# Carrying the softmax sums of a two-branch attention kernel by DMA, with paired V products and a new static order

## The chip, the cores and the metric

The kernel runs on one core of one Trainium2 chip. The metric is the device time of one execution in microseconds (us). Engines: PE is TensorE (matmul), PEld its weight loads, DVE is VectorE, ACT is ScalarE, POOL is GpSimd, SP is SyncE, which here only issues DMAs. Every ratio below is the mean time of one kernel's fast runs over the mean of the other's fast runs of the same rounds on the same chip, so it is not quite the ratio of the medians that are quoted. On one core a run counts as "slow" when it lies more than 1.5% above the fastest run of the same kernel. Such runs are left out of the ratios; where they matter I say how many there were. Here the slow runs are mostly those with the most time at half clock, so leaving them out can favour the kernel that has more of them.

## The reference, cut to what matters

```python
def reference(A_x, A_wqkv, A_w_phi, A_wo, B_x, B_wqkv, B_wo, gate_w):   # S=2048, D=512, 32 heads of 16
    # branch A: linear attention with a softmax feature map, per head
    phi_q = concat([softmax(q @ w_phi), softmax(-(q @ w_phi))]);  phi_k the same of k
    o_A = (phi_q @ (phi_k.T @ v)) / (phi_q @ sum(phi_k) + 1e-6)
    # branch B: ordinary softmax attention, 32 heads, 2048 x 2048 scores each
    p = softmax((q @ k.T) * 16 ** -0.5);  o_B = p @ v
    g = sigmoid((x * gate_w).sum(-1, keepdims=True))
    return g * (o_A @ A_wo) + (1 - g) * (o_B @ B_wo)                        # x = A_x in both branches
```

The cost is branch B: 32 blocks (4 query chunks x 8 head groups), each of 64 score tiles of 128 x 512, 2048 tiles in all. Every score has to go through an exponential.

## The kernel before: the parts that matter

The program is a list of operations with dependencies, estimated durations and priorities. Code in the kernel (`layout`) lays them out in time when the program is built, and each engine then gets its instructions in that fixed order, with semaphore waits only for true dependencies.

Most score tiles are exponentiated by ACT, in calls of two or three PSUM banks. 416 of them (`DN` per block) are instead approximated on DVE by integer arithmetic, in groups of four: D1 evicts each score tile from PSUM with the exponent bits in place, D2 and D3 split mantissa and exponent bits, D4 multiplies; in 32 of the 104 groups D4 runs on POOL (the range below names 34 numbers, two of which lie beyond the last group):

```python
ACTIVE = (0.64, 0.66, 0.60, 0.54)            # PE activity below which filler matmuls are planned
POOL_GROUPS = tuple(range(8, 110, 3))        # groups whose D4 runs on POOL
...
    add(0.72, lambda e: e.tensor_scalar(... 0x007F, 0x3F00, bitwise_and, bitwise_or), ..., "D2", ...)
    add(0.72, lambda e: e.tensor_single_scalar(... 0x7F80, bitwise_and), ..., "D3", ...)      # ops[-1].lock = True
    if g["n"] not in POOL_GROUPS:
        add(1.24, lambda e: e.tensor_tensor(t, t, m, ALU.mult), ..., "D4")
    else:
        for q in range(4):
            ops.append(P.add("pool", 1.0, ..., lambda e, q=q: e.tensor_tensor(quarter(t, q), ...), ...))
            ops[-1].lock = True
```

When the plan finds that PE streamed matmuls for less than a share `ACTIVE` of the last 3.4 us, it puts one or two filler matmuls, whose result nobody reads, in front of the next score product:

```python
    if op.room and t > 20.0 and active < ACTIVE[1]:
        op.extra = min(op.room, 1 if active > ACTIVE[2] else 2)
        ...
    elif op.tight and t > 20.0 and active < ACTIVE[3]:
        op.extra = 1
...
    def fn(e):                                # a score product for one exponential call
        for _ in range(op.extra):
            e.matmul(psS[:, ...], lhsT=ident[:], rhs=xT[:, 0, 0:NQ], start=True, stop=True)   # filler
        for m, t in enumerate(ts):
            ins = qk_mm(e, t, psS[:, ...])
```

The V products of a block collect in PSUM bank `psO`, with the sum of weights as one more row (a column of ones in `vaug`). At the end of each block DVE transposes the bank, takes a reciprocal, multiplies, and after every second block transposes back:

```python
    P.add("dve", 0.69, -50, lambda e: e.transpose(Tf[:, bb, :], psO[:]), ...)
    P.add("dve", 0.25, -40, lambda e: e.reciprocal(rd[:, bb, :], tv[:, :, DH]), ...)
    P.add("dve", 0.48, -40, lambda e: e.tensor_tensor(tbv, tv[:, :, 0:DH], rd..., ALU.mult), ...).lock = True
    if par == 1:
        P.add("dve", 0.72, -40, lambda e: e.transpose(oT[:, qc % 2, r, :], TB[:]), ...)
```

The softmax here doesn't subtract the row's maximum and nothing guards it: scores larger than these inputs give would overflow.

## Time and profile before

| | before |
|---|---|
| median of the first 3 runs | 807.58 us (807.06 to 808.99) |
| profiled span, mean granted PE clock | 805.6 us, 0.979 |
| ACT busy | 97% |
| exact exponential calls | 653, 750.6 us busy |
| ACT waiting for score products | 12.2 us in 17 waits |
| filler matmuls in front of score products | 133 |

The page of the kernel before: busy time and share of each engine, then the span in 40 slices (busy tenths; PEclk is the granted PE clock in tenths), then the chain of work that ended last, then the costliest group of instructions (count, busy us, mean ns, idle time before it and what ended that).

```profile
PE 741.4 (92%) x5890; PEld 229.8 (29%) x5959; DVE 691.4 (86%) x1120; ACT 778.3 (97%) x724; POOL 231.7 (29%) x188
...
PE   8999999989998999998899988998989999998889
...
DVE  3488879878766898898999999999999999989995
ACT  5899999999999999999999999999999999988996
...
PEclk9799999999999999999999999999999999978999
...
ACT 76%; PE 17%; DVE 6%; issue 1%; POOL 1%
ACT E_t L779 73%; PE psS L687 4%; PE psO L792 4%; ACT EA_t L960 3%; PE psS L534 2%; PE psM L534 2%; PE psS L704 1%; DVE Tx_t L749 1%; DVE vA_t L749 1%; DVE WB_t L759 1%; POOL WAT_t L767 1%; PE psM L454 1%; DVE vA_t L761 1%; DVE Tx_t L764 0%
...
L779 ACT ACTIVATE E_t<-psS 128x1536 bf16<-128x1536 f32 (+1 forms) x653 | 750.6, 1356 | 13.1 <-PE psS L687 10.0
```

ACT is busy from the first tenth to the last, and its exponentials are 73% of the chain that ended last. This is an ACT-bound kernel, and only the places where ACT waits can be won. The next lines are the waits of ACT for score products (total us, times, longest), the fillers' weight loads (the count is the number of fillers), and the core's mean clock.

```profile
ACT E_t L779 <- PE psS L687: 10.0, 13, 2.1
...
ACT E_t L779 <- PE psM L687: 2.2, 4, 0.9
```

```profile
L704 PEld LDWEIGHTS psS<-xT_t,ident_t x133: 95/96/118, 25.8 to 782.6; 128*128 128x128 bf16 x133
```

```profile
core 0: 805.6 us, clock 0.979
```

The granted clock takes only two values in these records, 1 and 0.5 (five stretches at 0.5 in this run), so the time at half clock is 2 x (1 - mean clock) x span: here 2 x 0.021 x 805.6 = 34 us. In these three windows (busy us of PE, PEld, DVE, ACT, POOL, then the granted clock) a dip ends in ACT waiting:

```profile
700.00:705.00 5.00, 4.03 (x31) 1.00 (x29) 5.00 (x8) 4.89 (x5) 0.90 (x1) 1.00 0.01 3
705.00:710.00 5.00, 3.73 (x17) 0.87 (x16) 4.86 (x7) 4.01 (x4) 4.42 (x4) 0.89 0.00 0
710.00:715.00 5.00, 5.00 (x19) 0.80 (x17) 2.90 (x6) 3.83 (x4) 0.00 (x0) 0.50 0.00 0
```

PE is busy only 3.73 of 5 us, then runs at half clock, and ACT, which needs PE's score products, falls to 3.83 us busy.

### The profile page before, as it was taken

The page shows a single profiled execution, that of the slowest core. Times are in us where ns is not written, and L with a number is a line of the kernel's source. Part 1 is how long each engine was busy: PE and PEld are TensorE (multiplying, and loading weights), DVE is VectorE, ACT ScalarE, POOL GpSimd, SP SyncE. Part 2 cuts the span into 40 slices and gives each one's busy share as a digit, 9 for nine tenths or more (in the row PEclk, how much of TensorE's full clock was granted, in tenths as well). Part 3 has the DMA queues.
Part 4 walks back from the last instruction along what each step waited for, and adds up shares of the span by engine and source line. Part 5 has one row for each costly group of instructions (what it writes and reads, how often), then busy time and mean ns, then how long its engine had stood idle before and what let it go on. Part 6 is the DMA issues. An engine that isn't in the chain of part 4 may idle for free.

```text
span 805.6 us, 14035 instructions
## 1 busy us (share of the span) xinstructions
PE 741.4 (92%) x5890; PEld 229.8 (29%) x5959; DVE 691.4 (86%) x1120; ACT 778.3 (97%) x724; POOL 231.7 (29%) x188
## 2 busy tenths in 40 slices
PE   8999999989998999998899988998989999998889
PEld 4323332333323232222232222322222222212223
DVE  3488879878766898898999999999999999989995
ACT  5899999999999999999999999999999999988996
POOL 5000022252443132522323333242222422342222
PEclk9799999999999999999999999999999999978999
DMA  6600000000100000000000000000000000000000
GB/s 125 138 2 2 1 1 2 1 1 1 53 1 2 1 7 14 1 9 1 1 1 2 1 2 1 1 14 2 15 1 1 4 4 14 8 0 1 1 1 27
DMA packets 18958, 9.30 MB, mean 12 GB/s; under 512 B 13264, under 2 KB 18896, under 8 KB 18896
## 3 DMA queue, kind: packets, MB, share of 16 engines
q1 hardware_dynamic: 17408, 7.74, 4.0%
q8 instruction: 46, 0.75, 0.4%
q10 hardware_dynamic: 1104, 0.66, 0.3%
q0 software_dynamic: 384, 0.02, 0.1%
q14 instruction: 16, 0.13, 0.1%
HBM read 3.69 MB, written 2.10 MB: 7 GB/s over the span
## 4 chain that ended last, share of the span: by engine, by line
ACT 76%; PE 17%; DVE 6%; issue 1%; POOL 1%
ACT E_t L779 73%; PE psS L687 4%; PE psO L792 4%; ACT EA_t L960 3%; PE psS L534 2%; PE psM L534 2%; PE psS L704 1%; DVE Tx_t L749 1%; DVE vA_t L749 1%; DVE WB_t L759 1%; POOL WAT_t L767 1%; PE psM L454 1%; DVE vA_t L761 1%; DVE Tx_t L764 0%; PE psM L1101 0%
## 5 line engine op out<-in xcount | busy, mean ns | idle before, releaser
L779 ACT ACTIVATE E_t<-psS 128x1536 bf16<-128x1536 f32 (+1 forms) x653 | 750.6, 1356 | 13.1 <-PE psS L687 10.0
L687 PE MATMUL psS<-qz_t,kTB_t 32*128 32x512 bf16 x1831 | 278.5, 391 | 43.8 <-ACT E_t L779 32.8
L792 PE MATMUL psO<-E_t,vaug_t 128*32 128x512 bf16 (+1 forms) x1632 | 242.8, 396 | 0.0
L687 PEld LDWEIGHTS psS<-qz_t,kTB_t 32*128 32x128 bf16 x1831 | 68.2, 91 | 270.6 <-ACT E_t L779 201.0
L767 POOL TENSOR_TENSOR Tx_t<-Tx_t,WB_t 128x512 bf16<-128x512 bf16 x44 | 53.8, 1253 | 144.4 <-DVE WAT_t L761 43.9
L792 PEld LDWEIGHTS psO<-E_t,vaug_t 128*32 128x32 bf16 (+1 forms) x1632 | 56.5, 93 | 129.1 <-issue 125.2
L749 DVE TENSOR_SCALAR Tx_t<-psM 128x512 int16<-128x512 f32 x103 | 70.5, 684 | 23.6 <-PE psM L687 21.7
L767 POOL TENSOR_TENSOR vA_t<-vA_t,WB_t 128x512 bf16<-128x512 bf16 x44 | 53.2, 1238 | 122.6 <-DVE WB_t L759 51.1
L687 PE MATMUL psM<-qz_t,kTB_t 32*128 32x512 bf16 x217 | 84.9, 391 | 2.4 <-DVE Tx_t L749 0.6
L792 PE MATMUL psO<-vA_t,vaug_t 128*32 128x512 bf16 (+1 forms) x304 | 76.4, 389 | 0.0
L749 DVE TENSOR_SCALAR Tx_t<-psS 128x512 int16<-128x512 f32 x85 | 57.9, 681 | 7.1 <-PE psS L687 4.3
L749 DVE TENSOR_SCALAR vA_t<-psS 128x512 int16<-128x512 f32 x71 | 48.4, 682 | 6.6 <-PE psS L687 4.4
L965 DVE TENSOR_REDUCE stat_t<-EA_t 128x64 f32<-128x1024 bf16 x32 | 38.8, 1214 | 16.7 <-ACT EA_t L960 16.4
L969 POOL TENSOR_TENSOR phiK_t<-EA_t,stat_t 128x1024 bf16<-128x1024 bf16 x16 | 33.2, 2080 | 65.1 <-DVE stat_t L967 65.1
L767 POOL TENSOR_TENSOR phiQ_t<-phiQ_t,WoA_t 128x512 bf16<-128x512 bf16 x16 | 18.0, 1154 | 116.7 <-DVE phiQT_t L761 116.7
L792 PE MATMUL psO<-Tx_t,vaug_t 128*32 128x512 bf16 (+1 forms) x188 | 51.4, 383 | 0.0
L767 POOL TENSOR_TENSOR WAT_t<-WAT_t,WB_t 128x512 bf16<-128x512 bf16 x24 | 29.8, 1269 | 64.2 <-DVE WB_t L759 21.6
L749 DVE TENSOR_SCALAR vA_t<-psM 128x512 int16<-128x512 f32 x65 | 44.5, 685 | 4.1 <-PE psM L687 3.1
L704 PE MATMUL psS<-xT_t,ident_t 128*128 128x512 bf16 x101 | 37.4, 413 | 8.7 <-ACT E_t L779 6.5
L969 POOL TENSOR_TENSOR phiQ_t<-EA_t,stat_t 128x1024 bf16<-128x1024 bf16 x16 | 32.3, 2021 | 43.3 <-DVE stat_t L967 43.3
L792 PE MATMUL psO<-WAT_t,vaug_t 128*32 128x512 bf16 (+1 forms) x156 | 44.1, 402 | 0.0
L764 DVE TENSOR_TENSOR Tx_t<-Tx_t,WB_t 128x2048 bf16<-128x2048 bf16 x24 | 29.1, 1212 | 0.1
(177 smaller groups left out, 939.3 us busy)
## 6 DMA issues: line engine op xcount, KB each, us to landing
out_dram<-WvA_t SPq DMA_DIRECT2D x14, 128.0 KB, 1.7
WB_t<-in_B_wqkv_dram SPq DMA_DIRECT2D x3, 384.0 KB, 4.5
WvA_t<-in_A_wqkv_dram SPq DMA_DIRECT2D x1, 512.0 KB, 4.1
WoA_t<-in_A_wo_dram SPq DMA_DIRECT2D x1, 512.0 KB, 3.6
WoB_t<-in_B_wo_dram SPq DMA_DIRECT2D x1, 512.0 KB, 4.6
phiK_t<-in_A_x_dram SPq DMA_DIRECT2D x2, 128.0 KB, 2.7
phiK_t<-in_A_x_dram ACTq DMA_DIRECT2D x2, 128.0 KB, 3.0
WB_t<-in_B_wqkv_dram SPq DMA_DIRECT2D x2, 128.0 KB, 3.9
```

Source lines behind the costliest of these rows:

```text
L454: ins = e.matmul(psM[:], lhsT=Ebuf[:, 0, 0:128], rhs=Ebuf[:, 0, 0:512], start=True, stop=True)
L534: return [lambda e, ap, i=i: e.matmul(ap, lhsT=lhs[i], rhs=rhs[i], start=(i == 0), stop=(i == len(lhs) - 1)) for i in range(len(lhs))]
L687: return e.matmul(bank, lhsT=kT_B[32 * i:32 * i + 32, hg // 2, 128 * kt:128 * (kt + 1)], rhs=qz[32 * i:32 * i + 32, (b // 8) % 2, hg, :], ...
L704: e.matmul(psS[:, 512 * base:512 * (base + 1)], lhsT=ident[:], rhs=xT[:, 0, 0:NQ], start=True, stop=True)
L749: ops.append(drain(f, mm, "dve", 0.70, d_prio(d), lambda e, ap, q=q: e.tensor_scalar(quarter(t, q).bitcast(I16), ap, EXPB, 0.0, op0=ALU.ad ...
L764: add(1.24, lambda e: e.tensor_tensor(shaped(t, m), shaped(t, m), m, ALU.mult), [g["m"]], tk, "D4")
L767: ops.append(P.add("pool", 1.0, d_prio(g["ts"][0]) - 5.0, lambda e, q=q: e.tensor_tensor(quarter(t, q), quarter(t, q), quarter(m, q), ALU. ...
L779: op = P.add("act", 0.051 + 0.4267 * n, 0.0, lambda e: e.activation(Ebuf[:, j // 2 % EPAIRS, 1536 * (j % 2):1536 * (j % 2) + 512 * n], psS ...
L792: return e.matmul(psO[32 * i:32 * i + w, :], lhsT=vaug[:, kt, VW * h:VW * h + w], rhs=rhs, start=start, stop=stop, tile_position=(0, 32 * ...
L960: ins = e.activation(EA[:, b, :].rearrange("p (g s c) -> p s g c", s=2, c=64)[:, sgn, :, :], ap.rearrange("p (g c) -> p g c", c=64), ACTF. ...
L965: P.add("dve", 1.22, prio, lambda e: e.tensor_reduce(stat[:, b, 1, :], e3, AX.X, ALU.add), reads=[("EA", b)], writes=[("ss", b)], name=f"s ...
L969: P.add("pool", 2.0, prio, lambda e: e.tensor_tensor(dst.rearrange("p (g f) -> p g f", f=DH), e3, stat[:, b, 1, :].unsqueeze(2).to_broadca ...
```

## The change

The intent is to take work off DVE and PE and to spend the room on a tighter order:

- Sums of weights: for 30 of 32 blocks DVE only copies `psO` to SBUF. The sum rows go to DRAM by DMA and come back in a compact form (128 x 16), DVE takes one reciprocal per pair of blocks, DMA carries it out and back as a broadcast, and POOL does the quotient (128 x 512).
- Q masks: one DVE eviction instead of two masked ones; the odd and even rows are sorted out by eight small DMAs.
- Score groups end with their block (all `DN` even, groups of four or two); `DN` sums to 422; 32 groups have D4 on POOL (`PN`).
- V products of two calls are issued as a pair (`PV_SETS`), and more matmuls may ride on others that use other rows or columns of PE (`want`; in the traces, score products that ride start 0.003 to 0.007 us after the other).
- New tuning numbers, among them lower thresholds for fillers (`ACTIVE`).

```diff
-DN = (0, 8, 10, 13, 11, 9, 13, 11, 3, ...)                 # sums to 416
+DN = (0, 12, 12, 14, 10, 14, 6, 10, 8, ...)                # sums to 422
-ACTIVE = (0.64, 0.66, 0.60, 0.54)
+ACTIVE = (0.56, 0.52, 0.46, 0.2)
-T_PRIO = -10.0
+T_PRIO = 20.0
+PV_SETS, PV_FROM = 2, 0
-POOL_GROUPS = tuple(range(8, 110, 3))
+PN = (0, 0, 0, 2, 0, 0, 1, 2, 1, 0, 3, ...)                # sums to 32
...
-                    want = {"qk": "dq", "pv": "term"}[last_pe]
+                    want = {"qk": "dq", "dq": "dq", "pv": "term", "term": "term"}[last_pe]
...
+        drain(f, mm, "dve", 0.69, prio, lambda e, ap: e.tensor_single_scalar(qz[:, c, 2 * r, :], ap, QSCALE, ALU.mult), ...)
+        moves(f"qo{c}{r}", lambda e: [e.dma_start(qz[o, c, 2 * r + 1, :], qz[o, c, 2 * r, :]) for o in z(1)], 4, ...)
+        moves(f"qe{c}{r}", lambda e: [e.dma_start(qz[o, c, 2 * r, :], qz[y, c, 2 * r + 1, :]) for ...], 4, ...)
...
+        if b < NB - 2:
+            P.add("dve", 0.69, -50, lambda e: e.tensor_copy(Tf[:, par, :], psO[:]), ..., name=f"ev.{b}")
+            moves(f"ld{par}", lambda e: e.dma_start(ld[par], Tf[16 - par::32, par, :]), 1, ...)
+            moves(f"lq{par}", lambda e: e.dma_start(Lq[:, par, :], ld[par].rearrange("i (a c) -> (i a) c", c=16)), 1, ...)
+            if par == 1:
+                moves("mg", lambda e: [e.dma_start(Tf[32 * i + 16:32 * i + 32, 0, :], Tf[..., 1, :]) for i in range(4)], 4, ...)
+                P.add("dve", 0.35, -40, lambda e: e.reciprocal(rd[:], Lq[:]), ...)
+                moves("lr", lambda e: e.dma_start(lr.rearrange(...), rd[:]), 1, ...)
+                moves("rb", lambda e: [e.dma_start(Rb[...], lr[t, i].unsqueeze(0).to_broadcast([16, D])) ...], 8, ...)
+                P.add("pool", 1.1, -40, lambda e: e.tensor_tensor(oT[:, qc % 2, r, :], Tf[:, 0, :], Rb[:], ALU.mult), ...).lock = True
...
-        add_pv(j)
+        held.append(j)
+        if (j + PV_FROM) % PV_SETS == PV_SETS - 1 or j == NS - 1:
+            for k in held:
+                add_pv(k)
+            held = []
```

## The prediction

> **What bounds the kernel now.** The engine-busy table gives ScalarE (ACT) 778.3 of 805.6 us (97%), PE 92%, DVE 691.4 us (86%), POOL 29%. The chain of waits that ended last is 73% exact exponentials. Back to back, one exponential call ends 1.34 us (1536 columns) or 0.92 us (1024) after the previous one (end-to-end distances in the trace). 653 calls at the mean of 1.13 are 737 us; 32 feature-map exponential pairs at 0.98 us (timeline) are 31 us. The first call starts at 11.9 us; after the last some 9 us remain. That makes 789 us, so only about 16 us of the span are stalls inside the exponential stream: by windows, 4-5 us before 50 us, 7 us in 700-750, the rest scattered. In 705-720 ACT starves because PE waits for DVE evictions, then the granted clock falls to 0.50 (windows) and matmuls take 0.6 us instead of 0.39.[...]
>
> **What the change does.**
> 1. Approximated tiles 416 -> 422, exact ones 1632 -> 1626, calls 653 -> 651: -2.5 us on ACT, the only work taken off the bounding engine.
> 2. DVE: per-block normalisation now costs 56 us (transpose 0.70 x32, reciprocal 0.24 x32, product 0.46 x32, second transpose 0.70 x16). For 30 of 32 blocks it becomes one PSUM copy (about 0.68, estimate from equal-sized evictions) plus a reciprocal per pair: estimate -28 us. Q masks: 30 evictions of 0.74 become 15: -11 us. Added: 6 tiles, ten more, smaller groups, two fewer groups with the product on POOL: +10 us. Net about -30 us, DVE 82-83%.
> 3. POOL: 15 quotients of 128x512 float (about 1.2 us, estimate from the 1.15-1.27 us products) +18 us, two product groups less -10 us, zeroing of qz about +8 us at the start. Not critical.
> 4. DMA: chains of five or six hops at about 2 us (output stores land in 1.7 us[...]). With pads 15-20 us per pair of blocks, against 50 us for a pair: hidden.
> 5. Paired V products: PE goes QK, QK, PV, PV rather than alternating. In the timeline, starts are 0.32 us apart at a change of kind against 0.215 within one kind; some 650 changes less are up to 68 us of PE time, an estimate. The lower thresholds put fewer filler matmuls in, so the granted clock may dip.
>
> **On the critical path:** 2.5 us surely, plus the part of the 16 us of stalls that slack on DVE and PE removes: I take about 6. The other freed DVE and PE time becomes idle time.
>
> **Predicted time:** 807.6 - 2.5 - 6.5 = 798.5 us; range 792.5 to 807. About 789 us is the floor unless head or tail shrink, so faster by over 2% (below 791.4) is unlikely: 0.06; within 2% 0.90; slower 0.04.
>
> **What would show it.** ACT busy near 775 us, still 97%; 651 exponential calls; DVE about 660 us; fewer and shorter ACT waits on PE; chain of waits still ~73% exponentials; fewer QK/PV changes in PE's timeline; Q copies and chains landing well before their readers.
>
> **What would make it wrong.** A low granted clock in long stretches from fewer fillers; a block's PSUM copy waiting because the DMA chain or the POOL quotient is late; DMA waits on the SP queue in the first 50 us delaying Q; POOL quotients slowing DVE[...]; or the new order removing stalls also at the head, which would go below 792.

Three passages of the record that no trace or run of this case shows are cut at their marks. None of them is a term of the sum, which stays 807.6 - 2.5 - 6.5 = 798.5 us. The about 2 us for each DMA hop in point 4 is the author's estimate, the 1.7 us of the output stores rounded up. The +8 us for zeroing `qz` in point 3 was an estimate as well; the two instructions that do it took 2.7 and 3.5 us in the changed kernel.

## More of the kernel before

Operations marked `lock` on DVE and POOL are kept apart *in the plan*. No semaphore enforces it on the chip:

```python
    if op.lock and max(lock_end[o] for o in lock_end if o != e) > t + 1e-9:
        pass                                  # not picked at this time
```

## The result, and the profile after

| | before | after |
|---|---|---|
| median, 4 runs each | 807.32 us (804.70 to 808.99) | 829.38 us (826.27 to 831.63) |
| ratio of the fast runs | 1 | 1.0274 (95% interval 1.0227 to 1.032): slower |
| profiled span | 805.6 us | 824.5 us |
| mean clock; time at half clock | 0.979; 34 us | 0.934; 109 us |
| exact calls | 653 | 651 |
| fillers | 133 | 49 |
| DVE held up behind POOL (see below) | 15 us, 21 times | 27 us, 36 times |

The page of the changed kernel, the lines that answer to those above:

```profile
PE 735.7 (89%) x5823; PEld 225.9 (27%) x5892; DVE 682.2 (83%) x1085; ACT 778.1 (94%) x722; POOL 261.7 (32%) x205
...
PE   8899999999989898988899988888888988988988
...
DVE  3688778876885687697789889999999999989986
ACT  5999999997999999999899899999999999989996
...
PEclk9999999997989979999799699999999989978799
...
ACT 56%; DVE 20%; PE 19%; issue 2%; SPq 1%; POOL 1%; DMA 0%
ACT E_t L818 53%; PE psO L832 6%; PE psS L722 6%; DVE Tx_t L784 5%; PE psS L550 3%; ACT EA_t L1027 3%; DVE WB_t L799 3%; DVE vA_t L801 2%; DVE vA_t L784 2%; DVE WAT_t L784 1%; PE psM L722 1%; DVE Tx_t L804 1%; SPq L445 1%; PE psM L550 1%; D
...
L818 ACT ACTIVATE E_t<-psS 128x1536 bf16<-128x1536 f32 (+1 forms) x651 | 749.6, 1315 | 32.5 <-PE psS L722 30.1
```

The number of calls is as planned, and DVE and PE have less to do. But the chain that ended last is now only 53% exponentials, 20% of it is DVE, and PEclk shows digits of 6 to 8 in 9 of the 40 slices, against 3 before. The waits of ACT, the fillers and the clock:

```profile
ACT E_t L818 <- PE psS L722: 30.1, 45, 2.1
...
ACT E_t L818 <- PE psM L722: 1.7, 5, 0.5
```

```profile
L739 PEld LDWEIGHTS psS<-xT_t,ident_t x49: 95/96/115, 28.3 to 773.4; 128*128 128x128 bf16 x49
```

```profile
core 0: 824.5 us, clock 0.934
```

ACT waits for score products 31.8 us instead of 12.2, and the time at half clock is 2 x 0.066 x 824.5 = 109 us instead of 34. The changed kernel's own plan is 780.2 us, shorter than the 784.8 us of the kernel before (both computed by the kernels' scheduling code when the program is built). So the loss is not in the length of the plan; the chip departs from it.

One place shows how. The first fence holds DVE and the second POOL between 183 and 187 us of the changed kernel (start, duration, line, what it does); L1034 is the reciprocal that the feature-map product L1036 needs, L799 is D2 and L801 is D3:

```profile
183.30 0.54 DVE L1034 RECIPROCAL stat_t<-stat_t 128x64 f32<-128x64 f32 x1
183.76 0.36 DVE L799 TENSOR_SCALAR WoA_t<-Tx_t 128x1024 int16<-128x1024 int16 x1
184.03 2.15 DVE L801 TENSOR_SCALAR WoB_t<-Tx_t 128x1024 int16<-128x1024 int16 x1
186.10 0.68 DVE L784 TENSOR_SCALAR Tx_t<-psM 128x512 int16<-128x512 f32 x1
```

```profile
183.92 1.98 POOL L1036 TENSOR_TENSOR phiK_t<-EA_t,stat_t 128x1024 bf16<-128x1024 bf16 x1 [0.32 <-DVE stat_t L1034]
```

D3 took 2.15 us. It started 0.11 us after a POOL product and ended 0.28 us after that product did. The plan had them the other way round: D3 at 180.4 us, the product at 180.8 us. In the plan the product's inputs were ready and POOL was free 0.57 us before that; only the lock kept it back. The chip has no such lock, so the product started 0.08 us after its reciprocal ended, and D3 came second. That the POOL product held D3 up is read from these times and from e5 below, where the product starts after D3 has ended and D3 takes 0.41 us. By what means one holds the other up is not in the trace.

Next, PE in the same place (the last brackets are idle time and what ended it), and three windows: before, during, after.

```profile
186.84 0.60 PE L722 MATMUL psM<-qz_t,kTB_t 32*128 32x512 bf16 x1 [1.85 <-DVE Tx_t L784]
...
187.38 0.61 PE L832 MATMUL psO<-WoB_t,vaug_t 128*32 128x512 bf16 x2
```

```profile
180.00:183.40 3.40, 3.29 (x22) 1.09 (x20) 2.53 (x4) 3.40 (x5) 2.76 (x2) 1.00 0.14 39
183.40:186.60 3.20, 1.58 (x12) 0.32 (x9) 3.20 (x4) 3.20 (x5) 2.18 (x2) 1.00 0.01 3
186.60:196.80 10.20, 9.73 (x38) 1.80 (x38) 4.08 (x8) 6.29 (x7) 1.93 (x1) 0.50 0.31 100
```

PE had to wait 1.85 us for DVE's evictions, was busy 1.58 of 3.2 us, and then ran at half clock for 10.2 us, in which ACT was busy only 6.29 us. Late DVE, idle PE, half clock, waiting ACT: this is the chain to be tested.

Two sums over the traces help. First, *DVE held up*: for each DVE instruction, its time from the later of its start and its predecessor's end, less the lower quartile of its group (same line and shape), where over 0.15 us. All of it overlaps a POOL instruction, in both kernels. In the changed kernel the 36 instructions are D2, D3, D4 and one quotient product; no eviction from PSUM is among them. Second, *PE cover*: the share of a 3.4 us window in which some matmul is streaming columns, counting 0.213 us for 512 columns at full clock and twice that at half clock (an estimate from the starts of matmuls back to back in the traces, which lie 0.216 us apart at full and 0.427 us at half clock, medians). In the windows just before the clock falls, the cover is 0.32 to 0.47 in the kernel before (5 stretches) and 0.38 to 0.55 in the changed one (13 stretches). Full-clock windows have a median of 0.68 and 0.66. The half-clock stretches last 3.4, 6.8, 10.2 or 13.7 us in these two runs and all begin on one grid of 3.41 us within each; of the full-clock windows of this grid, 7 of 220 lie under 0.5 before and 23 of 203 after, and a fall follows 5 and 10 of these. So the changed kernel has more windows in the range where falls occur. It is a range and not an edge: 13 of the 23 were followed by no fall, and in e9, below, falls came at 0.54 to 0.64. Over all 16 traces a fall followed 22 of 40 windows with a cover of 0.40 to 0.45, 25 of 225 at 0.50 to 0.55, and one above 0.65. No pause of PE was longer than 1.06 us before and 1.85 us in the changed kernel. These covers are estimates; some matmul records are missing from the traces (the page of the kernel before counts 5890 matmuls and 5959 weight loads).

### The profile page after: what moved, and what is told of

The parts are those of the page before. It is cut to its first block, busy times and chain, and to the rows that moved or that the text cites. A ratio compares the mean times of both kernels' runs of the same rounds, so it can differ in the third digit from the quotient of the medians.

```text
span 824.5 us, 14390 instructions
## 1 busy us (share of the span) xinstructions
PE 735.7 (89%) x5823; PEld 225.9 (27%) x5892; DVE 682.2 (83%) x1085; ACT 778.1 (94%) x722; POOL 261.7 (32%) x205
## 4 chain that ended last, share of the span: by engine, by line
ACT 56%; DVE 20%; PE 19%; issue 2%; SPq 1%; POOL 1%; DMA 0%
ACT E_t L818 53%; PE psO L832 6%; PE psS L722 6%; DVE Tx_t L784 5%; PE psS L550 3%; ACT EA_t L1027 3%; DVE WB_t L799 3%; DVE vA_t L801 2%; DVE vA_t L784 2%; DVE WAT_t L784 1%; PE psM L722 1%; DVE Tx_t L804 1%; SPq L445 1%; PE psM L550 1%; DVE WAT_t L801 1%
## 5 line engine op out<-in xcount | busy, mean ns | idle before, releaser
L818 ACT ACTIVATE E_t<-psS 128x1536 bf16<-128x1536 f32 (+1 forms) x651 | 749.6, 1315 | 32.5 <-PE psS L722 30.1
L722 PE MATMUL psS<-qz_t,kTB_t 32*128 32x512 bf16 x1839 | 305.4, 406 | 53.9 <-ACT E_t L818 39.7
L832 PE MATMUL psO<-E_t,vaug_t 128*32 128x512 bf16 x1626 | 219.0, 411 | 0.1
L807 POOL TENSOR_TENSOR Tx_t<-Tx_t,WB_t 128x512 bf16<-128x512 bf16 x64 | 82.5, 1318 | 77.6 <-DVE WAT_t L801 52.4
L784 DVE TENSOR_SCALAR Tx_t<-psS 128x512 int16<-128x512 f32 x123 | 83.4, 678 | 20.5 <-PE psS L722 15.6
L1036 POOL TENSOR_TENSOR phiQ_t<-EA_t,stat_t 128x1024 bf16<-128x1024 bf16 x16 | 32.4, 2022 | 147.6 <-DVE stat_t L1034 145.2
L832 PEld LDWEIGHTS psO<-E_t,vaug_t 128*32 128x32 bf16 x1626 | 42.7, 95 | 95.9 <-issue 90.7
L1036 POOL TENSOR_TENSOR phiK_t<-EA_t,stat_t 128x1024 bf16<-128x1024 bf16 x16 | 31.5, 1970 | 67.7 <-DVE stat_t L1034 67.7
L832 PE MATMUL psO<-vA_t,vaug_t 128*32 128x512 bf16 x290 | 50.5, 404 | 0.0
L832 PE MATMUL psO<-Tx_t,vaug_t 128*32 128x512 bf16 x232 | 46.7, 395 | 0.0
L804 DVE TENSOR_TENSOR Tx_t<-Tx_t,WB_t 128x2048 bf16<-128x2048 bf16 (+1 forms) x35 | 39.4, 1125 | 0.1
L799 DVE TENSOR_SCALAR WB_t<-Tx_t 128x2048 int16<-128x2048 int16 (+1 forms) x51 | 36.7, 721 | 0.2
L807 POOL TENSOR_TENSOR WAT_t<-WAT_t,WB_t 128x512 bf16<-128x512 bf16 x24 | 27.4, 1173 | 25.0 <-DVE vA_t L801 23.3
L807 POOL TENSOR_TENSOR vA_t<-vA_t,WB_t 128x512 bf16<-128x512 bf16 x20 | 28.3, 1448 | 21.0 <-DVE vA_t L801 17.8
```

The costliest lines, as they stand in the source:

```text
L722: return e.matmul(bank, lhsT=kT_B[32 * i:32 * i + 32, hg // 2, 128 * kt:128 * (kt + 1)], rhs=qz[32 * i:32 * i + 32, (b // 8) % 2, hg, :], ...
L784: ops.append(drain(f, mm, "dve", 0.70, d_prio(d), lambda e, ap, q=q: e.tensor_scalar(quarter(tb, q).bitcast(I16), ap, EXPB, 0.0, op0=ALU.a ...
L799: add(0.72 if full else 0.45, lambda e: e.tensor_scalar(shaped(mi, mi), shaped(ti16, mi), 0x007F, 0x3F00, op0=ALU.bitwise_and, op1=ALU.bit ...
L804: add(1.24 if full else 0.72, lambda e: e.tensor_tensor(shaped(t, m), shaped(t, m), m, ALU.mult), [g["m"]], tk, "D4")
L807: ops.append(P.add("pool", 1.1, d_prio(g["ts"][0]) - 5.0, lambda e, q=q: e.tensor_tensor(quarter(t4, q), quarter(t4, q), quarter(m4, q), A ...
L818: op = P.add("act", 0.051 + 0.4267 * n, 0.0, lambda e: e.activation(Ebuf[:, j // 2 % EPAIRS, 1536 * (j % 2):1536 * (j % 2) + 512 * n], psS ...
```

## The experiments

Three reasons were on the table. **F**: too few fillers, so the clock falls. **C**: collisions of DVE and POOL make DVE late, PE idle, and the clock fall. **S**: the new structure stalls by itself (with the forms P, the paired V products, and D, the DMA chains with the quotient on POOL). All runs gave correct results. "Order untouched" means that an experiment alters the program after the plan is made, so that every engine keeps its sequence; the others are planned anew and get another order.

The table has the result of all runs, each against the kernel before on the same chip (fillers are those in front of score products; half clock is the range over all runs of the kernel). The recorded verdicts, which ask for a clear 2%, are slower for after, e3, e4 and e8, unclear for e1, e2, e11, e12 and e14, and same for the rest; below, an interval that leaves out 1 is read as a smaller difference.

| run | order | fillers | half clock, us | median us | ratio, 95% interval |
|---|---|---|---|---|---|
| after | - | 49 | 109 to 126 | 829.38 | 1.0274, 1.0227 to 1.032 |
| e1 after + gap fillers | kept | 192 | 16 to 65 | 828.15 | 1.0228, 1.0144 to 1.0312 |
| e2 before without fillers | kept | 0 | 103 to 130 | 822.87 | 1.0219, 1.0166 to 1.0272 |
| e3 after, old thresholds | new | 220 | 86 to 117 | 851.07 | 1.0536, 1.0458 to 1.0614 |
| e4 after, V products single | new | 30 | 161 to 207 | 852.43 | 1.0557, 1.0497 to 1.0617 |
| e5 after + POOL waits | kept | 49 | 74 to 115 | 815.38 | 1.0093, 1.002 to 1.0166 |
| e6 before + POOL waits | kept | 133 | 27 to 40 | 804.85 | 0.9973, 0.9924 to 1.0021 |
| e7 e5 + gap fillers | kept | 192 | 0 to 41 | 811.38 | 1.0022, 0.9943 to 1.0102 |
| e8 after, no D4 on POOL | new | 58 | 139 to 195 | 848.91 | 1.0477, 1.041 to 1.0545 |
| e9 e5 + targeted fillers | kept | 184 | 21 to 64 | 814.42 | 1.0096, 1.0069 to 1.0122 |
| e10 before + both | kept | 165 | 14 to 47 | 804.19 | 0.997, 0.9943 to 0.9997 |
| e11 e9, V products single | new | 107 | 37 to 64 | 820.62 | 1.0172, 1.013 to 1.0214 |
| e12 e9, old normalisation | new | 176 | 28 to 65 | 827.08 | 1.02, 1.0157 to 1.0244 |
| e13 e5 + light fillers | kept | 97 | 24 to 72 | 808.88 | 0.9967, 0.9917 to 1.0016 |
| e14 e9, old riding rules | new | 100 | 24 to 75 | 828.10 | 1.0173, 1.0114 to 1.0232 |

### e1: fillers into the gaps of the changed kernel

```diff
     P.layout()
+    for x, op, y in zip(pe, pe[1:], pe[2:]):     # neighbours on PE, at() is the planned start
+        if op.kind == "qk" and (op.room or op.tight) and at(op) - x.end + x.lat + at(y) - op.end + op.lat >= 0.32:
+            op.extra = max(op.extra, 1)
```

> The changed kernel with its instruction order untouched; only 143 filler matmuls are added (192 instead of 49), one in front of a score product wherever the kernel's own plan leaves the PE at least 0.32 us idle around it. Theory F (too few fillers, so the PE's granted clock falls to half): half-clock time falls from 109 us to under 50 us, mean clock from 0.93 to 0.97 or more, time from 829 to 795-812 us. Rival S (the new structure itself stalls: DMA chains, paired V products, GpSimd collisions): clock and time stay within 1% of the changed kernel, or get worse, since fillers only add PE work.

The clock did what theory F said, 0.971 in the profiled run with 48 us at half clock instead of 109. The time did not: 828.15 us. ACT still waited 29.7 us for `psS` (30.1 us without the fillers), as the clock slices and the wait of e1 show. So F alone falls. Either the clock does not matter, or the 143 fillers cost as much as they gave.

```profile
PEclk9999999999999999999599999997899998999999
```

```profile
ACT E_t L818 <- PE psS L722: 29.7, 52, 2.3
```

### e2: the kernel before without its fillers

```diff
     P.layout()
+    for op in P.ops:
+        op.extra = 0
```

> The kernel before, order untouched, with all 133 filler matmuls in front of its score products left out. Theory F: half-clock time rises from 34 us to about 100 us or more and the time from 807 to 820-835 us, so that the old structure loses as much as the changed kernel did. Rival S: less PE work and the same structure, so the time stays at 800-811 us.

Here less PE work made the kernel slower, 822.87 us, as F said and S did not. These are the core line, the clock slices and ACT's wait of e2:

```profile
core 0: 815.7 us, clock 0.937
```

```profile
PEclk9799999999999999799999989999989998968779
```

```profile
ACT E_t L779 <- PE psS L687: 17.3, 28, 2.1
```

Collisions were as before (14 us of DVE held up, 15 us before), so the clock matters by itself. That leaves e1 to be explained by the fillers' own cost.

### e3 and e4: old thresholds, and V products single, both planned anew

```diff
-ACTIVE = (0.56, 0.52, 0.46, 0.2)
+ACTIVE = (0.64, 0.66, 0.60, 0.54)      # e3
-PV_SETS, PV_FROM = 2, 0
+PV_SETS, PV_FROM = 1, 0                # e4
```

> The changed kernel with the filler thresholds of the kernel before (0.64, 0.66, 0.60, 0.54); it is planned anew with 220 fillers, and the kernel's own plan is 24 us longer (805 against 780). Theory F: clock 0.97 or more, and the time at 805-820 us, below the 829 of the changed kernel although its plan is longer. Rival S: the plan's 24 us come on top, about 850 us.

> The changed kernel with V products no longer paired (one set per score slot, planned anew, only 30 fillers, plan 784 us). Theory F: the fillers are as few as before, so it stays slow: 820-835 us with a mean clock of 0.92-0.95. Rival P (it is the pairing of V products, which makes long PE bursts and leaves the exponential waiting): time 800-812 us and clock back to 0.97 or more.

e3 came out at 851 us, where S had put it: the plan's 24 us came on top. It is no proof of S, because the new order brought a stall of its own: ACT waited 19 us for `psO` in two waits, which no other order has to that size. e4 was slower still, with 161 to 207 us at half clock, so pairing the V products is not what lost the time; unpairing them, with 30 fillers left and a new order, made it worse. A plan made anew changes too much at once. From here on the order was kept where possible.

### e5 and e6: POOL waits for DVE, in both kernels

```diff
     P.layout()
+    last = None
+    for op in sorted(P.order["dve"] + P.order["pool"], key=lambda o: o.pos):
+        if op.lock and op.eng == "dve":
+            last = op
+        elif op.lock and last is not None:
+            op.deps = op.deps + [last]      # POOL may not start before the DVE operation planned before it
```

> The changed kernel, order untouched; every GpSimd product or quotient now also waits (semaphore) for the last DVE score-term or quotient instruction that the kernel's plan starts before it, so that GpSimd can no longer start early and hold DVE up. Theory C (GpSimd and DVE hold each other up because the chip drifts from the plan; late DVE makes PE wait and the clock fall): excess DVE time falls from 27 us to under 12 us, PE waits on DVE from 20.6 us to about 10, half-clock time from 109 to under 70 us, time from 829 to 805-815 us. Rival F (fillers alone): DVE excess falls but half-clock stays at 90 us or more and the time at 820 us or more.

> The same waits in the kernel before. Theory C: its DVE excess falls from 15 us to under 6 us and its drift of 22 us from its plan by a third or more: 795-804 us, and faster than the kernel before by 0.5 to 1.5%. If the collisions cost nothing on the path, 804-808 us.

e5 recovered 14 of the 22 us: 815.38 us. DVE held up fell from 27.4 to 11.3 us, the pauses of PE (matmuls and weight loads idle for over 0.1 us) that DVE ended from 20.6 to 14.6 us, and the half-clock time from 109 us to 75 us in the profiled run (the core line of e5 is below). The pauses and the half clock fell less than the expectation had it. D3 at the place shown above now takes 0.41 us, and POOL's product waits for it (DVE, then POOL, of e5):

```profile
182.89 0.36 DVE L799 TENSOR_SCALAR WoA_t<-Tx_t 128x1024 int16<-128x1024 int16 x1
183.16 0.41 DVE L801 TENSOR_SCALAR WoB_t<-Tx_t 128x1024 int16<-128x1024 int16 x1
183.49 0.68 DVE L784 TENSOR_SCALAR Tx_t<-psM 128x512 int16<-128x512 f32 x1
```

```profile
183.66 1.93 POOL L1036 TENSOR_TENSOR phiK_t<-EA_t,stat_t 128x1024 bf16<-128x1024 bf16 x1 [0.83 <-DVE WoB_t L801]
```

```profile
ACT E_t L818 <- PE psS L722: 16.5, 28, 2.1
```

```profile
core 0: 808.7 us, clock 0.954
```

In the kernel before the same waits cut the held time from 15.0 to 8.5 us, yet the time only to 804.85 us, which is not clear of noise. That lies in the range that the expectation gave for collisions that cost nothing, and outside the one for C. The kernel before had fewer collisions and 84 fillers more; that these let it survive them is a reading, not shown. Theory C is shown for the changed kernel, where the order was kept and only waits were added, and not for the kernel before.

### e7 and e9: both repairs

e7 is e5 plus the fillers of e1. e9 is e5 plus 135 fillers placed by the planned PE cover:

```diff
+        if op.kind == "qk" and (op.room or op.tight) and not op.extra and gap >= 0.2 and min(
+                share(at(op) - k, at(op) - k + WINDOW) for k in (0.5, 1.7, 2.9)) < 0.62:
+            op.extra = 1
```

> The changed kernel with both repairs, the waits of e5 and the 143 added fillers of e1; order untouched. If both causes are real and add up: half-clock under 35 us, mean clock 0.98, time 795-808 us. If fillers cost PE time that is missing elsewhere (as e1 hints), it is not faster than e5.

> The changed kernel with the waits of e5 and 135 fillers more (184), each placed where the plan's matmul streams cover under 0.62 of a 3.4 us window and the plan leaves 0.2 us idle around the score product; order untouched. Theory C plus F (collisions and too little PE activity are the whole loss): half-clock under 25 us, time 795-806 us, at or below the kernel before. If something else in the structure costs time too: clock 0.98 or more and still 808 us or slower.

Neither beat the kernel before. e7 has two of its four runs at a clock of 1.000, with 806.35 and 806.25 us, beside 816.40 us at 0.981 and 820.47 us at 0.975. The same program, so the difference within it goes with the clock: 31 us at half clock for 10 us. But even wholly without half clock it stood at 806 us. e9 had 0.983 and still 812 to 816 us in its fast runs, the case that its expectation called "something else".

### e8: no score product on POOL

```diff
-PN = (0, 0, 0, 2, 0, 0, 1, 2, 1, 0, 3, ...)
+PN = (0,) * 32
```

> The changed kernel with all score products on DVE (none of 32 groups on GpSimd), planned anew: plan 792 us against 780, DVE 39 us busier, GpSimd left with feature maps and quotients. Theory C: loss over the plan falls from 47 us to 25-35 us, time 815-828 us although DVE has more to do. Rival S (pairing and DMA chains stall by themselves): the loss over the plan stays at 45 us or more, 837 us or slower.

848.91 us: my expectation for C was wrong. DVE held up did fall to 12 us, but a DVE with 39 us more work in the plan is late on its own account: it ended 24.4 us of PE's pauses, against 20.6 us in the changed kernel, and 139 to 195 us ran at half clock. The new order also made ACT wait 14.0 us for `psO`, so this run separates nothing cleanly. Taking the collisions away by giving the work back is no repair.

### e10: both repairs in the kernel before

The edit is that of e9 (165 fillers instead of 133).

> The kernel before with the same two repairs (165 fillers instead of 133, waits of e5). Both theories: half-clock from 34 to under 20 us, time 797-804 us, faster than the kernel before by 0.4 to 1.2%. If fillers only cost, 804-810 us.

804.19 us against 806.55 us, a ratio of 0.997 with an interval just under 1. With one run of six left out as slow, this is the only version of fourteen whose interval lies below 1. The times of its fast runs are 802.43 to 806.70 us. The slow run (814.67 us) had 47 us at half clock; with all six the mean is 805.9 us against 806.3 us of the kernel before. That it is faster is not shown.

### e11 and e12: V products single, and the old normalisation, on top of e9

e11 is e9 with `PV_SETS = 1`. e12 is e9 with `if b < 0:` in place of `if b < NB - 2:` in the normalisation (with the rows of `psO` and the output calls put back to match), so that all blocks go by DVE, and no sums by DMA and no quotient on POOL are left.

> e9 with V products unpaired (planned anew, plan 784 us, 107 fillers). If e4's 852 us came of clock and collisions alone, it now falls to 800-815 us, and pairing is worth a few us at most. If unpaired products cost PE time that is on the path with this plan's denser rides, it stays above 825 us.

> e9 with the normalisation of the kernel before on DVE (two transposes, reciprocal, product) for all blocks; no sums by DMA, no quotient on GpSimd; planned anew, plan 793 us against 780. Theory: the DMA form is not what loses time, it saves DVE about 25 us, so this one is slower than e9 by 5-20 us. Rival D (sums by DMA and the quotient on GpSimd are what stall the changed kernel): this one is faster than e9, near 795-803 us.

e11 fell from e4's 852 to 820.62 us, a little above its forecast range, and is 6 us slower than e9: this fits clock and collisions as most of e4's loss. e12 is 13 us slower than e9, where rival D wanted it faster, so D falls as the cause of the loss. How much carrying the sums by DMA gains is less sure: e12 has a new order, and its plan is 13 us longer too. DVE was busy 688.4 us in e12 and 668.0 us in e9, 20 us more. The DMA chain also never held up DVE or PE to speak of: in the changed kernel's trace, DVE waits for it 0.5 us in one wait, and PE never. Only POOL waits for it, and of DVE and PE a single wait of 0.7 us (after the head) is for POOL:

```profile
POOL oT_t L924 <- DMA Rb_t<-lr: 177.2, 13, 61.6
```

### e13 and e14: what was still open, the price of fillers and the denser packing

e13 is e9 with 0.54 in place of 0.62: 97 fillers instead of 184. e14 is e9 with the riding rules and `T_PRIO` of the kernel before, planned anew.

> e9 with fewer fillers: 97 instead of 184, only where the plan's streams cover under 0.54 of a 3.4 us window; order untouched, waits of e5. If a filler costs about as much as the half-clock time it saves (e5 and e9 both near 814 us), an intermediate number gives 806-812 us with 30-60 us of half-clock; if fillers beyond the changed kernel's own 49 are useless, 813-816 us; a version at 803 us or less would show that well placed fillers repair the rest.

> e9 with the riding rules and the term priority of the kernel before (only one kind of matmul may ride on a score or V product), planned anew: 100 fillers, plan 795 us, PE planned busy 716 us instead of 676. If the denser packing of PE is what leaves activity low, half-clock falls to under 35 us with fewer fillers than e9 and the loss over the plan from 34 us to near the 22 us of the kernel before: 813-820 us. If packing is harmless, the loss over the plan stays near 34 us: 827 us or more.

e13 gave 808.88 us over six runs (800.13 to 814.91), where the first branch of its expectation had it. Two runs are left out of the ratio as slow; with all six the mean is 808.6 us, so it is level with the kernel before (807.47 us), not ahead of it. Half as many fillers are better than 184. e14 came out where its expectation had it for harmless packing: with 100 fillers it spent 24 to 75 us at half clock, as much as e13 with 97, and its loss over its plan of 795 us stayed at 33 us. So nothing points to the denser packing of PE as what brings the half clock; but the order is new, and DVE was held up for 17.8 us against 10.6 us in e13.

### Putting the runs together

In each kernel with enough spread of its own, the runs lie on a line of time against half-clock time. e13's six runs go from 800.13 us at 24 us of half clock to 814.36 us at 72 us: 0.30 us for each us at half clock. A straight-line fit gives 0.28 for the changed kernel, 0.28 for e2, 0.35 for e5, 0.34 for e7 and 0.34 for 36 runs of the kernel before; over all kernels it lies between 0.28 and 0.42. I use 0.33 to take the half clock out of every run, by time - 0.33 x half-clock time. The result is an estimate, and an extrapolation over some 100 us for the changed kernel: with 0.28 it would be 796 us there instead of 790. It also takes the line within a kernel as what half clock costs. A disturbance that makes both a run longer and its clock lower was not ruled out.

| kernel | fillers | time less 0.33 x half clock |
|---|---|---|
| before | 133 | 796 |
| e2 before without fillers | 0 | 784 |
| after | 49 | 790 |
| e1 after + 143 fillers | 192 | 812 |
| e5 after + POOL waits | 49 | 787 |
| e13 e5 + 48 | 97 | 792 |
| e9, e7: e5 + 135, + 143 | 184, 192 | 806 |

Read this way, the half clock costs 0.33 x 117 = 39 us after (mean of its four runs) against 0.33 x 33 = 11 us before, and the rest is 790 against 796 us. These parts give 39 - 11 - 6 = 22 us, the measured loss, by construction: it is a split of the loss and not a test of it. The 6 us are no gain of the new structure either. The changed kernel has 84 fillers fewer, and the kernel before without any (e2) stands at 784 us. For a filler is not free: (812 - 790) / 143 = 0.15 us in e1, (806 - 787) / 135 = 0.14 us in e9, (796 - 784) / 133 = 0.09 us in the kernel before, where the plan was made around them (all three lie between 0.06 and 0.20 us if the slope is anywhere from 0.28 to 0.42). At these prices 84 fillers are 8 to 13 us, more than the 6. e1 bought 24 us of clock with 22 us of fillers. On this account the clock rose and the time stood still.

## Why the prediction was wrong, point by point

- **What bounds the kernel, and the 2.5 us.** Right on the bound: 651 calls, and ACT is still what all else serves. The 2.5 us are not shown: the calls' busy time fell by 1.0 us (750.6 to 749.6), and the 6 us by which the estimate without half clock is lower are no more than what the missing fillers are worth.
- **DVE about 30 us lighter.** Right in kind, too large in size, and partly hidden. DVE busy went from 691.4 to 682.2 us, 9 us. But busy time includes time held up behind POOL: less the 15.0 and 27.4 us, it went from 676 to 655 us, 22 us. e12 puts the normalisation at 20 us (forecast: 28).
- **POOL: "Not critical."** This step failed. (Its "two product groups less" was a slip too: both kernels have 32.) POOL's busy time was off the path, but its *starts* were not: a POOL instruction that began a little before a D2, D3, D4 or quotient product of DVE held it up for as much as 1.7 us here. The prediction named "POOL quotients slowing DVE" as a risk. The quotients took part in some 4 of the 27 us; most of it was the score products (19 us), which were there before (12 of 15 us). e5 shows that the collisions were worth 14 us.
- **DMA chains hidden.** Right: the hops whose landing the trace shows landed in 1.6 to 1.9 us (medians), no stall of DVE or PE to speak of came from them (0.5 us in one wait), and e12 without them is slower.
- **Paired V products.** Right that they help: unpairing cost 23 us in e4 and 6 us in e11, both planned anew. That PE slack would be worth something was wrong: the PE was not the limit except at half clock (ACT was busy 6.29 us of the 10.2 us above), and less PE work went with more of that (in e2 103 to 130 us).
- **"The lower thresholds put fewer filler matmuls in, so the granted clock may dip."** Named, and entered into the sum with nothing. This is the term that was mis-sized: 84 us more at half clock (117 instead of 33, means over runs), at 0.33 us each, is 28 us.
- **"the part of the 16 us of stalls that slack on DVE and PE removes: I take about 6."** This is the step that failed. It took slack for punctuality. With 84 fillers fewer, PE's windows were emptier (of the full-clock windows, 23 of 203 under a cover of 0.5 instead of 7 of 220; in e2, 133 fillers less brought 82 us more at half clock by themselves), and the plan's order was broken more often. ACT's waits for score products went from 12.2 to 31.8 us.

How much of the half clock comes from each of the two causes is not fully separated: e5 removes 28 us of 117 us by the waits alone (means), and fillers remove most of the rest at their own price. What made the new plan collide more often (21 to 36 times) was not tested by a run, but plan and trace together say much. In 25 of the 36 collisions, 22 of the 27 us, POOL went first where the plan had DVE first, and 23 of these POOL instructions had been kept back in the plan by the lock alone: inputs ready, POOL free. No drift is needed for that; such an instruction starts as soon as its semaphores let it (the product shown above, 0.08 us after its reciprocal ended). The new plan has 43 POOL starts that are delayed so, by 38.5 us in all; the plan before has 31, by 22.9 us. These are the starts that the waits of e5 hold back.

## What to carry to other kernels

A static order that keeps two engines apart is not kept by the chip where no semaphore carries it: here 23 POOL instructions whose inputs were ready went ahead of the DVE instruction planned before them, and a D3 of 128 x 1024 took 2.15 us behind one and 0.41 us without. Make the off-path engine wait for the one on the path (the waits of e5 cut the held time from 27.4 to 11.3 us and the time from 829 to 815 us), and check the duration of each instruction against its own group for being held up. Before taking work off an engine whose clock falls when it has less to do, as PE's did here (in e2, 133 fillers less, 82 us more at half clock), find the share of each window that its work covers; where windows sank into the range in which falls occurred (0.32 to 0.55 in the kernel before and the changed one), saved work came back as half clock, here at about a third of a microsecond for each microsecond (0.28 to 0.42, fitted). Fillers that are put in front of critical work had a price, an estimated 0.09 to 0.15 us each here, so put in as few as the clock demands.
